# The first transform of a convolution's input taken from raw x with scaled matrices, and its neighbours moved

## The chip, the core and the metric

The kernel runs on one core of a Trainium2 chip. Five engines work side by side, each through its own list of instructions in order: TensorE (PE, with its weight loads shown as PEld), VectorE (DVE), ScalarE (ACT), GpSimd (POOL) and SyncE (SP), which here only starts transfers. The metric is the device time of one execution in microseconds (us).

## What is computed

A row of 640 channels and 2048 positions goes through a state-space convolution and a gated feed-forward part, each behind a layer norm whose scale and shift come from a conditioning vector:

```python
mod = (_silu(c) @ w_mod).reshape(c.shape[0], 6, 1, -1)      # sa, ca, ga, sb, cb, gb
h = _layernorm(x) * (1 + ca) + sa
x = x + ga * A(h)                        # A: y = causal convolution of h with K, plus h * D_skip
h = _layernorm(x) * (1 + cb) + sb
x = x + gb * B(h)                        # B: (silu(h w1) * (h w3)) w2, 1728 wide
# K[d, l] = 2 Re sum_n C[d, n] dt[d] exp(A[d, n] dt[d] l), n = 128
```

All arithmetic is in 32-bit floating point. The convolution is done by transforms of length 4096.

## The kernel before

The first part works on five blocks of 128 channels (b = 0 to 4). For each block:

- **The filter K** is generated in eight chunks of 16 channels (`gen_tasks`, `gen_chunk`). POOL adds integer phases (`ph`), three multiplications make magnitudes (tasks `z0` to `z2`, function `size`, on POOL), ACT takes sines (`tr`), DVE multiplies both (`xx`, `yy`), PE sums over n into the bank `kps`, four small matmuls add `D_skip` at one position (`kps<-dsk`), and ACT copies the bank to `ks`.
- **The input h** is made from x (`h_tasks`): four loads of raw x per block (`xq`), a normalisation by row (`hn<-xq`, on ACT or DVE), a multiplication by the gain row and an addition of the shift row on DVE (`hn<-hn,rw`, `hb<-hn,rw`), a store to the DRAM buffer `hs`, and a load back in another order (`xb<-hs`).
- **A first transform** of both (`first_tasks`): eight banks each of `ps<-wk,xb` for h and `ps<-wk,ks` for K, each bank copied by ACT or DVE into a spectrum `sp`.
- **A second transform** (`spectra_tasks`): `fh` for h, `fk` for K, eight banks each. ACT copies `fh` to `hz`, DVE multiplies the two spectra (`product`, `both`), PE goes back over frequencies (`fz`), and ACT or DVE copies that to `zt`, which is stored to the DRAM buffer `zd`.

The product has two forms, chosen by block in `FORM = "AABBB"`. In form A one DVE instruction of 1024 elements makes four partial products and PE adds them up with eight matmuls a bank pair; in form B two multiplications of 512, then a subtraction and an addition of 256 on DVE leave four matmuls.

After the last block comes a border. The last inverse transforms are read back from `zd` (`iz`, `izb`), summed with x by PE and DVE (`iy`, `iyb`), normalised and turned (`tp`), and the feed-forward part begins (`gu`, later `X`, `c`, `acc`), in two passes over 14 tiles of w1, w3 and w2.

The order of the first part and of the border is set by a table of numbers, `ORDER`: each number is a task and a mark behind it picks the second of two engines that may do it. Each engine executes its instructions in that order, and so does the queue of SP, through which nearly all transfers are started. The transfers of x for the second half of the rows (`x<-in_x` into `x2[2]` and `x2[3]`) and of two matrices `wd` are started at the head of `ffn`.

Of the kernel before, what the change touches and what calls it, by code (L numbers as in the profile page):

```python
# [18 lines left out]
P = 128  # L19
# [15 lines left out]
1 80 78 81 79 82 83 150' 2 4 19 42 20 41 14 21 15 84 22 43 23 44 16 85 151 24 17 25 26 45 46 18 28 59 47 30 27 29 48 96 33 36 49  # L35
34 5 111 35 32 61 31 37 40 50 51 38 39 3 152' 153 156 6 7 8 52 53 62 60 157 154 10 91 158 155 159 167 168 89 86 120 93 87 95 107
54 121 13 310 105 109 98 169 171 113 172 173 110 106 90 174 55 102 100 88 56 114 176 118 177 183 179 66 170 117 178 184 185 57 104
58 64 187 188 108 175 99 189 180 181 67 186 192 194 9 115 193 103 190 160 92 199 200 201 101 97 203 11 195 68 202 161 182 204 191
215 122 123 208 65 63 209 196 197 69 205 206 210 116 94 207 211 219 112 138 124 127 198 162 212 71 213 128 134 400' 119 163 125
# [3 lines left out]
267 338 334 259 339 315 265 266 405 260 268 77 335' 409 72 147 148 149 0 550 340 272 273 269 274 270 271 261 275 322 330 279 276  # L43
555 283 280 281 288 341' 551' 262 282 284 285 323 286 331 290 552 289 553 318 277 326 556 319 287 291 327' 417 421 418 422 278 320
321 423 292 557 426 545 316 293 137 410 75 74 546 424 419 558 420 427 317' 428 547 548 328 413' 414 324 429 425 294 329 430 433
437 325 346 342 344 554 559 436 434 442 435 431 347 438 444 343 345' 443 348 350 365 352 439 549 440 441 432 445 449 450 451 452
# [4 lines left out]
505 496 517 1054 394 583' 510 570 518 515 654 652 529 516 530 531 574 810 373 809 1055 571 533 511 584 524 523 1056 522 572 575  # L51
519 811' 812 813 1058 1057 384 532 656' 539 585 512 520 534 573 535 538 525 540 576 395 1059 577 521 396 1060 588 1061 398' 566
1063 814 589' 536 537 567 526 1064' 1065 1066 568 580 569' 527 578 908 909 581 579 528 657 655 658 659 660 667 683 668 684 661 685
669 541 592 593' 542 1311 594 671 1068 1069' 676 1070 595 672 543 590 544 670 678 677 596 673 674 591 662 663 686 664 910 665 1071
815 597 586 820 675 679 587' 680 1062 1067 1072 687 821' 692 1312 1313 1314 699 824 598 681 818 600 1316 1315 825 688 693 819' 694
# [3 lines left out]
730 752 753 608 399 630 826 744 745 618 757 756 827 754 631 755 619 641 759 750 763 764 758 620' 760 766 765 767 768 746 769 770  # L59
# [13 lines left out]
1221 1127 907 1222 1122 1124 1125 1340 1341 1214 1223 1116 1228 1227 1128 1141 1229 1234 1232 1179' 1233 1177 1117 1129 1130 1119  # L73
# [132 lines left out]
class K:  # L206
# [1139 lines left out]
    def ffn(self):  # L1346

        W, X, v, w2 = self.first
        for b in (2, 3):
            self.load_x2(b)  # L1350
# [766 lines left out]
```

## Time and profile before

| | |
|---|---|
| time, median of 3 runs | 954.85 us (951.83 to 956.61) |
| span of the profiled execution | 950.6 us; the page gives no other time for it |
| busy: PE, DVE, ACT, POOL | 868.3, 684.2, 549.9, 342.1 us |
| instructions: PE, DVE, ACT, POOL | 8369, 1294, 1035, 371 |
| first `fh` of block 0 | 111.8 us |
| first matmul of the feed-forward part (`gu`) | 380.5 us |

How to read it: the first 380 us are the convolution, in which all four engines have work, and the remaining 570 us are the feed-forward part. A 32-bit matmul of the program stands as two records in the profile. A duration is from start to end of one instruction, and neighbours on an engine overlap a little, so a sum of durations is somewhat longer than the busy time.

### The profile page before, as it was taken

How to read it: one execution, taken by the hardware profiler on the slowest of the kernel's cores; microseconds unless marked ns; L12 is line 12 of the kernel's file. 1: busy time of each engine (PE TensorE's matmuls, PEld its weight loads, DVE VectorE, ACT ScalarE, POOL GpSimd, SP SyncE). 2: the span in 40 equal slices, each digit the busy share in tenths (PEclk: the TensorE clock that was granted, in tenths of full speed). 3: DMA queues.
4: the chain of work that ended last, by engine and by line, in shares of the span. 5: the costliest groups of instructions: out<-in, count | busy, mean ns of one | idle time of the engine just before them, and what ended most of it. 6: DMA issues, size and time to landing. Idle time of an engine off the chain costs nothing.

```text
span 950.6 us, 21218 instructions
## 1 busy us (share of the span) xinstructions
PE 868.3 (91%) x8369; PEld 686.4 (72%) x8369; DVE 684.2 (72%) x1294; ACT 549.9 (58%) x1035; POOL 342.1 (36%) x371
## 2 busy tenths in 40 slices
PE   1267999999999986999999999999999999999997
PEld 0035858777888863787777778888788888888775
DVE  7997999999989878896776775657556555555422
ACT  6688999989797732754444444544444444443412
POOL 0899989998998500011111211000121212120000
PEclk9997999999999997999999999999999999999999
DMA  9976553524143598654533422375432222221374
GB/s 201 266 225 171 158 150 107 138 80 127 47 119 84 143 241 209 170 175 149 154 113 121 139 67 87 94 238 171 126 92 83 83 84 83 84 84 31 111 230 127
DMA packets 110508, 127.42 MB, mean 134 GB/s; under 512 B 10568, under 2 KB 90696, under 8 KB 109128
## 3 DMA queue, kind: packets, MB, share of 16 engines
q1 hardware_dynamic: 109032, 125.27, 46.7%
q8 instruction: 66, 1.08, 0.5%
q10 hardware_dynamic: 1376, 0.79, 0.3%
q14 instruction: 34, 0.28, 0.1%
HBM read 95.89 MB, written 30.15 MB: 133 GB/s over the span
## 4 chain that ended last, share of the span: by engine, by line
PE 73%; DVE 9%; ACT 8%; DMA 5%; issue 2%; POOL 1%; SPq 1%; ACTq 0%; DVEq 0%; POOLq 0%
PE c L151 19%; PE acc L151 18%; PE X L151 12%; PE ps L151 5%; PE kps L151 4%; PE fz L151 4%; PE fk L151 3%; PE fh L151 3%; PE gu L151 2%; ACT tr L151 1%; DVE xb L151 1%; PE iy L151 1%; DMA sp<-zd 1%; DMA zd<-zt 1%; DVE yy L151 1%
## 5 line engine op out<-in xcount | busy, mean ns | idle before, releaser
L151 PE MATMUL acc<-ah,w 128*128 128x512 f32 x560 | 173.4, 395 | 1.9 <-DMA w<-w2d 1.2
L151 PEld LDWEIGHTS acc<-ah,w 128*128 128x128 f32 x560 | 103.8, 188 | 25.3 <-ACT ah L598 1.8
L151 PE MATMUL acc<-al,w 128*128 128x512 f32 x260 | 102.3, 393 | 0.0
L599 DVE TENSOR_TENSOR wl<-s,wh 128x256 fp32r<-128x256 f32 x92 | 39.0, 424 | 67.0 <-ACT wh L598 66.5
L775 POOL TENSOR_TENSOR s<-wr 128x256 f32<-128x256 f32 x22 | 16.4, 743 | 184.8 <-DMA wr<-in_w 104.7
L598 ACT ACTIVATE wh<-s 128x256 fp32r<-128x256 f32 x92 | 37.6, 409 | 78.0 <-PE X L151 58.1
L151 POOL TENSOR_TENSOR ph<-p,p 128x1024 int32<-128x1024 int32 x40 | 78.8, 1970 | 6.2 <-ACT tr L151 5.6
L598 ACT ACTIVATE wh<-wr 128x256 fp32r<-128x256 f32 x92 | 38.4, 418 | 56.1 <-PE X L151 42.4
L776 POOL TENSOR_TENSOR s<-s,wr 128x256 f32<-128x256 f32 x22 | 17.1, 776 | 131.5 <-issue 128.0
L151 DVE TENSOR_TENSOR yy<-yy,tr 128x512 f32<-128x512 f32 (+1 forms) x60 | 56.5, 944 | 2.9 <-ACT tr L151 2.1
L836 ACT ACTIVATE t<-g 128x512 f32<-128x512 f32 x44 | 27.8, 632 | 52.9 <-DVE g L800 52.9
L151 PEld LDWEIGHTS acc<-al,w 128*128 128x128 f32 x260 | 48.9, 188 | 11.3 <-DVE al L599 0.4
L151 ACT ACTIVATE tr<-ph,hpi 128x512 f32<-128x512 f32 x80 | 54.5, 688 | 3.3 <-DVE yy L151 1.3
L151 DVE TENSOR_TENSOR xx<-tr,xx 128x512 f32<-128x512 f32 x80 | 54.2, 681 | 2.9 <-ACT tr L151 2.5
L805 DVE SCALAR_TENSOR_TENSOR g<-t,g 128x512 f32<-128x512 f32 x48 | 33.7, 701 | 31.3 <-ACT t L836 29.3
L151 PE MATMUL kps<-yy,xx 128*32 128x64 f32 x1920 | 37.8, 231 | 18.3 <-DVE xx L151 14.2
L151 PE MATMUL fz<-fp,wz 64*128 64x512 f32 x224 | 54.0, 608 | 0.3 <-DVE fp L151 0.3
L151 PEld LDWEIGHTS kps<-yy,xx 128*32 128x32 f32 x1920 | 32.8, 114 | 27.1 <-issue 11.1
L599 DVE TENSOR_TENSOR wl<-wr,wh 128x256 fp32r<-128x256 f32 x92 | 40.2, 438 | 15.1 <-ACT wh L598 15.0
L151 PE MATMUL ps<-wk,xb 128*64 128x128 f32 x640 | 47.2, 294 | 2.8 <-DVE hb L151 1.1
L151 ACT ACTIVATE tr<-ph 128x512 f32<-128x512 int32 x80 | 47.2, 599 | 2.3 <-DVE yy L151 1.8
L598 ACT ACTIVATE ah<-h 128x512 fp32r<-128x512 f32 x26 | 16.4, 632 | 53.1 <-PE acc L151 53.1
(454 smaller groups left out, 2442.3 us busy)
## 6 DMA issues: line engine op xcount, KB each, us to landing
w<-w2d SPq DMA_DIRECT2D x42, 640.0 KB, 3.9
wr<-in_w SPq DMA_DIRECT2D x50, 320.0 KB, 3.9
zd<-zt SPq DMA_DIRECT2D x40, 256.0 KB, 3.2
w2d<-w SPq DMA_DIRECT2D x14, 640.0 KB, 3.5
xs<-in_x SPq DMA_DIRECT2D x16, 320.0 KB, 11.9
hs<-hb SPq DMA_DIRECT2D x20, 256.0 KB, 3.2
xb<-hs SPq DMA_DIRECT2D x20, 256.0 KB, 4.8
iz<-zd SPq DMA_DIRECT2D x32, 160.0 KB, 4.2
```

The source lines that it names most:

```text
L151: self.prev = self.k.order(f(*a, **kw), self.prev)
L598: self.nc.scalar.activation(H, v, AF.Copy)
L599: eng.tensor_tensor(Lo, v, H.bitcast(F32), op=ALU.subtract)
L775: eng.tensor_tensor(s[0], u[:, 0:2], u[:, 2:4], op=ALU.add)
L776: eng.tensor_tensor(s[1], s[0], g[:, 0:2], op=ALU.subtract)
L805: V.scalar_tensor_tensor(g, th, 1.0, g, op0=ALU.add, op1=ALU.mult)
L836: tanh = lambda o, i: A.activation(o, i, AF.Tanh, scale=0.5)
```

## The change

- **h from raw x.** `h_norm`, `h_mul` and `h_add` are gone. Raw x is the moving operand of PE, 32 positions at a time, and the transform matrix is multiplied by the rows' 1/std (`hw`, `hl`; tasks `hw0`, `hw1`, `hl0`, `hl1`, once for all blocks). A second, accumulating matmul adds the mean and the shift. Each of the 20 tasks `h{b}.{i}.m` issues 32 matmuls (`hp`), on four groups of 32 rows of the array, into two banks. ACT or DVE copies each bank to `hb`, two transfers store it to `hs`, and four loads per block bring the result straight to the place of the spectrum. There are no banks `ps<-wk,xb` and no copies of them.
- **The gain** of block 0 is multiplied to x on DVE (four instructions). For the other blocks it goes into K's parameters and into `D_skip` (tasks `mv`, `gain`, `pr`, `rw` instead of the rows and `fold`).
- **The skip per half block.** Ten small additions on POOL or DVE (`g{b}.d0`, `g{b}.d1`) replace the matmuls `kps<-dsk`. The first transform of K waits for them, so for four chunks at a time.
- **Form B for all blocks.** `FORM` is `"BBBBB"`.
- **Two engines to choose from** for `z0` to `z2` (14 of 120 are on DVE now) and for the head of a table.
- **The border.** The loads `izb` are all started by SP (half of them were by ACT). `x2[2]` and `wd[2]` are loaded as tasks of the border, `x2[3]` and `wd[3]` within the first pass.
- **A new `ORDER`** for all of it.

```diff
@@ -32,67 +32,66 @@
 ORDER = """
-1 80 78 81 79 82 83 150' 2 4 19 42 20 41 14 21 15 84 22 43 23 44 16 85 151 24 17 25 26 45 46 18 28 59 47 30 27 29 48 96 33 36 49
...
+1 2 6 79 81 3 82 20 15 5 83 85 84 21 16 43 154' 42 80 22 155 23 24 17 25 18 19 115 44 29 7 31 62 45 30 32 60 26 9 40 157 27 46 158 8
...
-FORM = "AABBB"
+FORM = "BBBBB"
...
-    def h_make(self, pc, b):
+    def h_first(self, pc, b, bank):
...
         for j in range(4):
+            for n in range(2):
+                for g in range(4):
+                    p, q = slice(32 * g, 32 * g + 32), 64 * (g % 2)
+                    self.nc.tensor.matmul(bank[g // 2][q:q + 64, j * P:j * P + P], (self.hl if n else self.hw)[p, 4 * b + j, :],
+                                          self.hr[p, pc * P:pc * P + P] if n else x[p, j, :], start=(n == 0), stop=(n == 1),
+                                          skip_group_check=True, tile_position=(32 * g, q))
+    def h_store(self, pc, b, c):
+        hb = self.hb.pop((pc, b, c))
+        to = self.hs[pc].rearrange("f (g s) d -> g f s d", g=4)
+        for q in range(2):
+            self.nc.sync.dma_start(to[2 * c + q, :, 4 * b:4 * b + 4], hb[64 * q:64 * q + 64].rearrange("p (s d) -> p s d", s=4))
...
-            for q in range(4):
-                g = slice(32 * q, 32 * q + 32)
-                nc.tensor.matmul(kps.rearrange("p (e b) -> p e b", b=64)[g, :, 63], self.ident[g, g], self.dsk[g, d0 // P, d0 % P // 4:d0 % P // 4 + 4],
-                                 start=False, stop=True, skip_group_check=True, tile_position=(32 * q, 32 * q))
...
+        def skip(e, h):
+            k = self.ks[b][:, 16 * h:16 * h + 16, 63]
+            self.eng(e).tensor_tensor(k, k, self.dsk[:, b, 16 * h:16 * h + 16], op=ALU.add)
...
-                add(n + f"z{i}", "POOL", 1.03, lambda c=c, i=i: ch[c][1](i), [n + "ph", f"exp{b}"] + ([f"mag{b}"] if i == 2 else [n + "z0"] if i else []),
+                add(n + f"z{i}", ("POOL", "DVE"), (1.03, .6), lambda e, c=c, i=i: ch[c][1](e, i), [n + "ph", f"exp{b}"] + ([f"mag{b}"] if i == 2 else [n + "z0"] if i else []),
...
-            add(n + "n", ("ACT", "DVE"), (1.89, 1.66), lambda e, i=i, place=place: self.h_norm(b, i, place(), e), [n + "l", "hscale"], t, take=[(bank, 1)],
-            add(n + "x", "DVE", .61, lambda i=i: self.h_mul(b, i), [n + "n", "fold"], t + .1)
-            add(n + "a", "DVE", .61, lambda i=i: self.h_add(b, i), [n + "x"], t + .2, take=[("hz", 1)], give=[(bank, n + "n")])
+            add(n + "m", "PE", 1.95, lambda i=i: mm(i), [n + "l", "rw0", "rw1", "hw0", "hx0", "hx1"] + ([n + "x"] if b == 0 else []), t + .2,
+            for c in range(2):
+                add(n + f"e{c}", ("ACT", "DVE"), (.48, .61), lambda e, i=i, c=c: self.h_out(b, i, c, pk[i][c], e), [n + "m"], t + .2, take=[("hz", 1)],
...
+            add(f"h{b}.f{k}", "SP", 0, lambda k=k: self.h_fetch(b, k), [f"h{b}.{i}.o{c}" for i in range(4) for c in range(2)] + old, W["h"](b, 4), dma=[524288])
...
-                    (self.nc.scalar if h else self.nc.sync).dma_start(z["b", b][h * 64:h * 64 + 64, pr], zv[:, t0:t0 + 4, cut:])
+                    self.nc.sync.dma_start(z["b", b][h * 64:h * 64 + 64, pr], zv[:, t0:t0 + 4, cut:])
```

Three places of the order carry the prediction. **The first** is PE at the first `fh` of block 0. Before, it stands behind the ninth chunk of K (`kps`) in the program's order:

```order
L151 MATMUL ps_1227<-wk,ks_133 64x4x16x2 x8
L151 MATMUL ps_1236<-wk,ks_133 64x4x16x2 x8
L151 MATMUL ps_1245<-wk,ks_133 64x4x16x2 x8
L151 MATMUL kps_1260<-x_94,xx_1098 32x64 x32
L151 MATMUL kps_1260<-dsk,ident 32x4 x4
L151 MATMUL fh_1304<-sp,wb 64x128 x8
L151 MATMUL fk_1313<-sp,wb 64x128 x8
```

In the change it stands behind the eleventh chunk, between two tasks that already transform h of block 1 (`hp`, weights from `xb`, moving operand `xq` or the row `rw`):

```order
L154 MATMUL hp<-xq_1353,xb 64x128 x4
L154 MATMUL hp<-rw,xb 64x128 x4
L154 MATMUL kps_1492<-yy_1136,xx_1135 32x64 x32
L154 MATMUL fh_1534<-sp,wb 64x128 x8
L154 MATMUL fk_1548<-sp,wb 64x128 x8
L154 MATMUL hp<-xq_1399,xb 64x128 x4
L154 MATMUL hp<-rw,xb 64x128 x4
```

So the second transform of block 0 has moved two chunks later, and work of block 1 ahead of it. **The second** place is DVE among the products of block 0. Before, form A's product of 1024 elements stands beside the arithmetic of h (`hn`, `hb`) and the sines' products (`yy`, `xx`):

```order
L151 TENSOR_TENSOR fp_1588<-fk_1517,hz_1577 128x4x256
L151 SCALAR_TENSOR_TENSOR yy_1529<-yy_1529,tr_192_1579 128x16x32
L151 TENSOR_TENSOR yy_1529<-yy_1529,tr_192_1579 128x16x32
L151 TENSOR_TENSOR hn<-hn,rw 128x512
L151 TENSOR_TENSOR xx_1528<-tr_192_1599,xx_1528 128x512
L151 TENSOR_TENSOR hb_1626<-hn,rw 128x512
```

In the change a product of block 0 is two multiplications and two sums, and a magnitude (`xx<-late`) that POOL made before stands among them:

```order
L154 TENSOR_TENSOR fp_1607<-fk_1548,hz_1557 128x2x2x128
L154 TENSOR_TENSOR fk_1548<-fk_1548,hz_1557 128x2x2x128
L154 TENSOR_TENSOR fp_1607<-fp_1607,fk_1548 128x256 x2
L154 SCALAR_TENSOR_TENSOR yy_1487<-yy_1487,tr_192_1600 128x16x32
L154 TENSOR_TENSOR yy_1487<-yy_1487,tr_192_1600 128x16x32
L154 TENSOR_TENSOR xx_1612<-late 128x512
```

The arithmetic of h has left DVE here, and more of the products' work has come to it. **The third** is the queue of SP at the border. Before, behind the last store of `zd`, it starts two of the four loads of each `izb` (ACT starts the others), a weight tile and then x:

```order
L151 DMA izb_5365<-zd 64x4x128 x2
L151 DMA izb_5395<-zd 64x4x128 x2
L151 DMA wr_1_5400<-in_w 128x5x128 x2
L594 DMA x_5384<-in_x 32x2560 x4
L594 DMA x_5385<-in_x 32x2560 x4
```

In the change it starts all eight, with a weight row between the two groups:

```order
L154 DMA izb_5546<-zd 64x4x128 x4
L154 DMA w2r_5587<-in_w 128x640
L154 DMA izb_5600<-zd 64x4x128 x4
L154 DMA x_5584<-in_x 32x2560
L154 DMA wr_1_5613<-in_w 128x5x128
```

The loads of x are spread out behind it, and four starts of `izb` have moved from ACT to SP.

More of the change, by code (lines that the diff above doesn't have):

```diff
@@ L1300, in tail_tasks @@
         load_down(2)
+        add("lwd2", "SP", 0, lambda: self.nc.sync.dma_start(self.wd[2], self.t_wd[:, 8:12]), ["change"], -20, dma=[262144])
+        for q in range(4):
+            s = slice(q * 32, q * 32 + 32)
+            add(f"lx2.{q}", "SP", 0, lambda q=q, s=s: self.nc.sync.dma_start(self.x2[2][s], self.xv[q, :, 8:12, :]), ["border"], -20, dma=[327680])
         down_split(2, 60)
@@ L1359, in groups @@
             more = m < 12
+            if p == 0 and m == 4:
+                self.load_x2(3)
             if more:
@@ L1548, in border @@
             self.x2 += [self.fp.tile([P, 4, D], F32, name=f"x2{i}") for i in (2, 3)]
-        plan.add("change", None, 0, change, [f"g{b}.7.p", f"g{b}.7.r"] + [f"h{b}.{i}.x" for i in range(4)], 0, own=True)
+        plan.add("change", None, 0, change, [f"g{b}.7.p", f"g{b}.7.r"], 0, own=True)
         self.tail_tasks(border, cut)
@@ L1920, in param_tasks @@
             if k:
-                c = chain(f"pc{k}.", end, n, {0: [b]}, prio + .3 + k * later)
+                c = chain(f"pc{k}.", end, n, {0: [b], len(end) - 1: ["gain"]}, prio + .3 + k * later)
             else:
@@ new lines, in early_tasks, with spread @@
+        add("mv", "PE", .4, columns, ["m"], 21, take=[("f2", 1)], give=[("hz", "m")])
+        add("gain", "DVE", 1.6, gain, ["mv", "dt", "hc"], 21, give=[("f2", "mv")], port=True)
+        def spread(i):
+            o = pr["r", i] = ps.tile([P, 512], F32, name=f"prow{i}", tag="f", bufs=3)
+            for k in range(4) if i == 0 else (4,):
+                for g in range(4):
+                    nc.tensor.matmul(o[32 * g:32 * g + 32, k % 4 * P:k % 4 * P + P], gc[:, k], self.ident, start=True, stop=True, tile_position=(0, 32 * g))
+            if i:
+                nc.tensor.matmul(o[:, P:2 * P], bc(gc[:, 0, 0], 1, P), self.ident, start=True, stop=True)
+                for q in range(4):
+                    g = slice(32 * q, 32 * q + 32)
+                    nc.tensor.matmul(o[g, 2 * P:3 * P], hc[g, 65:97], de[g].rearrange("p b e -> p (b e)"), start=True, stop=True, tile_position=(32 * q, 32 * q))
@@ new lines, in keep @@
+        def keep(i):
+            if i == 0:
+                return A.activation(rwf[:, :512], pr["r", 0], AF.Copy)
+            A.activation(rwf[:, 512:768], pr["r", 1][:, :256], AF.Copy)
+            A.activation(self.dsk[:, 1:].rearrange("p b e -> p (b e)"), pr["r", 1][:, 256:384], AF.Copy)
+        for i in range(2):
+            add(f"pr{i}", "PE", .9, lambda i=i: spread(i), ["gain"], 21, take=[("f2", 1)])
+            add(f"rw{i}", "ACT", .55, lambda i=i: keep(i), [f"pr{i}"], 21, give=[("f2", f"pr{i}")])
@@ new lines, in rows_of, with ends @@
+        def rows_of(i):
+            V.tensor_tensor((self.hw, self.hl)[i], bc(self.h_rs[i], 2, 64), bc(hc[:, :64], 1, NJ), op=ALU.mult)
+        for i in range(2):
+            add(f"hw{i}", "DVE", 1.13, lambda i=i: rows_of(i), ["hscale", "hc", "pc0", "pc1.8"], 21)
+        pl = {}
+        def ends(i):
+            pl[i] = ps.tile([P, 512], F32, name=f"hl{i}", tag="f", bufs=3)
+            for g in range(4):
+                p = slice(32 * g, 32 * g + 32)
+                for n, (o, r) in enumerate(((65, self.hl[p, 8 * i:8 * i + 8]), (64, bc(hc[p, :64], 1, 8)))):
+                    nc.tensor.matmul(pl[i][p], hc[p, o:o + 32], r, start=(n == 0), stop=(n == 1), skip_group_check=True, tile_position=(32 * g, 32 * g))
@@ L2062, in early_tasks, with lower @@
+        def lower(i):
+            A.activation(self.hl[:, 8 * i:8 * i + 8], pl[i].rearrange("p (j c) -> p j c", j=8), AF.Copy)
+        for i in range(2):
+            add(f"hl{i}", "PE", 1.0, lambda i=i: ends(i), ["hw1"], 21, take=[("f2", 1)])
+            add(f"hx{i}", "ACT", .48, lambda i=i: lower(i), [f"hl{i}"], 21, give=[("f2", f"hl{i}")])
+        add("wb", "SP", 0, lambda: nc.sync.dma_start(self.wb, self.t_wb), ["mr4", "lat1", "turn0", "turn1"], 60, dma=[2097152])
         w = {}
```

252 lines of the change are left out of this document (125 added, 127 removed), and 66 rows, old and new, of the table ORDER.

## The prediction

> **What bounds the kernel now.** I read the span first, then the busy time by stage, cut where PE starts a chunk of K: the ninth, the 25th and the last of the forty.
>
> ```profile
> span 950.6 us, 21218 instructions
> 110.54 1.17 PE L151 MATMUL kps<-x,xx 128*32 128x64 f32 x64
> 235.03 1.17 PE L151 MATMUL kps<-yy,xx 128*32 128x64 f32 x64
> 327.69 1.17 PE L151 MATMUL kps<-yy,xx 128*32 128x64 f32 x64
> ```
>
> The columns of the next rows are the stretch, its length, the busy time of PE, its weight loads, DVE, ACT and POOL, the granted clock, and the DMA share.
>
> ```profile
> 0.00:83.90 83.90, 31.27 (x465) 17.02 (x465) 73.69 (x151) 64.64 (x127) 55.80 (x71) 0.94 0.83 225
> 83.90:110.54 26.64, 24.21 (x497) 21.50 (x489) 23.61 (x40) 24.34 (x45) 25.50 (x27) 0.94 0.63 169
> 110.54:235.03 124.49, 118.74 (x2371) 94.09 (x2369) 117.84 (x171) 116.74 (x199) 113.36 (x111) 1.00 0.45 119
> 235.03:327.69 92.66, 92.09 (x2074) 77.45 (x2073) 86.15 (x144) 76.59 (x133) 80.40 (x76) 1.00 0.35 94
> 327.69:354.20 26.51, 24.02 (x384) 19.39 (x385) 18.27 (x37) 9.87 (x20) 0.00 (x0) 1.00 0.98 232
> 354.20:380.50 26.30, 17.85 (x94) 10.07 (x93) 21.09 (x73) 5.93 (x10) 0.63 (x1) 0.74 0.89 211
> ```
>
> From 110 to 235 us PE is busy 95%, DVE 95%, ACT 94% and POOL 91%: nothing is slack, and an engine that gets faster alone gains little. From 235 to 328 us PE is full (99%) with DVE at 93% behind it. Before 84 us PE is mostly idle and DVE leads (88%). Behind 380.5 us comes the feed-forward part, 570 us that the change does not touch but for transfers started elsewhere. So the gain, if there is one, is made between 84 and 328 us, and it needs less work on PE and on DVE at once. What DVE waited for from 100 to 330 us was small:
>
> ```profile
> DVE fp L151 <- PE fk L151: 4.3, 8, 1.3
> DVE yy L151 <- ACT tr L151: 2.6, 7, 0.8
> DVE xx L151 <- ACT tr L151: 1.9, 4, 1.4
> ```
>
> **What the change does to PE.** These rows show the matmuls that go, and what stands next, so that start to start gives the cost on PE.
>
> ```profile
> 129.43 3.70 PE L151 MATMUL fz<-fp,wz 64*128 64x512 f32 x16
> 133.06 1.13 PE L151 MATMUL fh<-sp,wb 128*64 128x128 f32 x16
> ...
> 198.19 1.17 PE L151 MATMUL kps<-yy,xx 128*32 128x64 f32 x64
> 199.29 0.24 PE L151 MATMUL kps<-dsk,ident 32*32 32x4 f32 x8
> 199.46 1.15 PE L151 MATMUL fk<-sp,wb 128*64 128x128 f32 x16
> 200.43 1.18 PE L151 MATMUL ps<-wk,xb 128*64 128x128 f32 x16
> 201.55 1.17 PE L151 MATMUL kps<-x,xx 128*32 128x64 f32 x64
> ...
> 238.89 1.99 PE L151 MATMUL fz<-fp,wz 64*128 64x512 f32 x8
> 240.81 2.06 PE L151 MATMUL fh<-sp,wb 128*64 128x128 f32 x32
> ```
>
> - Form B in blocks 0 and 1: an inverse transform takes 133.06 - 129.43 = 3.63 us in form A and 240.81 - 238.89 = 1.92 us in form B. Eight of them change: 8 x 1.71 = **-13.7 us**.
> - The skip: 199.46 - 199.29 = 0.17 us per chunk, 40 chunks: **-6.8 us**.
> - h's first transform: forty banks at 201.55 - 200.43 = 1.12 us go, 45 us, and twenty tasks `hp` of 32 matmuls, 64 records, come. No row shows four groups of 32 rows with long moving operands. Two rows bound it, and two show how much runs side by side:
>
> ```profile
> L151 PE MATMUL fz<-fp,wz 64*128 64x512 f32 x224 | 54.0, 608 | 0.3 <-DVE fp L151 0.3
> L151 PE MATMUL ps<-wk,xb 128*64 128x128 f32 x640 | 47.2, 294 | 2.8 <-DVE hb L151 1.1 <-DVE fp L151 0.6 <-DVE sp L151 0.6
> L151 PE MATMUL kps<-dsk,ident 32*32 32x4 f32 x320 | 9.7, 180 | 0.0
> ```
>
>   `ps` works on two halves of the array's columns: 16 records in 1.12 us are 8 steps of 0.14 us. `fz` works on two halves of its rows, in different banks; 224 records of 608 ns in 54.0 us, so neighbours overlap. With four row groups at once a task `hp` is 16 steps, 16 x 0.14 = 2.2 us. It can't be less than 1.1 us, in which the 64 records of a `kps` are issued, and with only two groups at once it is 32 x 0.14 = 4.5 us. I take 2.2 us, as the two row groups of `fz` are nearest: 20 x 2.2 = 44 us for 45, **-1 us** (ends -23 and +45).
>
> The gain's small matmuls replace four of the same kind where PE is idle: 0. Sum for PE: **-21 us**.
>
> The Trainium skill bears on `hp` in TensorE: Matmul & The Clock Gate, section Why this matters for your kernels: four tiles of 32 rows ran concurrently and gained 3.07 times, not four. By that a task would be an estimated 2.2 x 4 / 3.07 = 2.9 us and PE's sum -8 us. No run here shows it yet.
>
> **What it does to DVE, ACT and POOL.** Counts are those of the two programs, durations are the rows' means.
>
> ```profile
> L151 DVE TENSOR_TENSOR fp<-fk,hz 128x1024 f32<-128x1024 f32 x16 | 19.5, 1218 | 1.4 <-PE fk L151 1.1 <-ACT hz L151 0.3
> L151 DVE COPY sp<-ps 128x512 f32<-128x512 f32 x28 | 18.9, 681 | 2.9 <-PE ps L151 2.7
> L151 DVE TENSOR_TENSOR fp<-fp,fk 128x256 f32<-128x256 f32 x48 | 17.9, 415 | 0.5
> L151 DVE TENSOR_TENSOR fp<-fk,hz 128x512 f32<-128x512 f32 x24 | 16.5, 688 | 9.4 <-PE fk L151 8.0 <-ACT zt L151 0.9 <-ACT wh_u L151 0.3
> L151 DVE TENSOR_TENSOR hn<-hn,rw 128x512 f32<-128x512 f32 x20 | 13.9, 693 | 0.4
> L151 DVE TENSOR_TENSOR hb<-hn,rw 128x512 f32<-128x512 f32 x20 | 13.7, 686 | 0.5
> L151 DVE TENSOR_SCALAR hn<-xq,rs_y_h,rs_n_h 128x128 f32<-128x128 f32 x28 | 11.5, 412 | 0.9
> L151 DVE TENSOR_SCALAR step<-pS 128x128 int32<-128x128 int32 x3 | 0.7, 270 | 0.0
> ```
>
> DVE loses 32 normalisations (the 28 shown and four like them, 13.2 us), the multiplications and additions of h (27.6), sixteen products of form A (19.5), eleven of 28 copies to `sp` (7.5) and some 5 us of smaller work: 73 us. It gets sixteen pairs of form B's multiplications (32 x 0.69 = 22.0) and 32 sums (32 x 0.415 = 13.3), 14 magnitudes from POOL (9.6), seven copies of `hp` (4.8), 25 shifts of tables less four (some 5), four multiplications of x (2.8), two of the transform matrix (2.4), and some 18 tiny instructions of `gain`, between 0 and 0.4 us each, at the shifts' 0.27 us 5 us. Sum 65 us: **-8 us** (ends -13 and -6).
>
> ```profile
> L151 ACT ACTIVATE sp<-ps 128x512 f32<-128x512 f32 x52 | 30.0, 590 | 9.8 <-PE ps L151 9.7
> L151 ACT ACTIVATE hn<-xq,rs_n_h,rs_y_h 128x128 f32<-128x128 f32 x36 | 16.6, 461 | 1.0
> L151 POOL TENSOR_TENSOR yy<-late 128x512 f32<-128x512 f32 x22 | 23.2, 1074 | 0.0
> ```
>
> ACT loses 48 normalisations at 0.461 us (22) and 29 copies to `sp` at 0.59 (17) and gets 33 of `hp` (19.5): about **-19 us**. POOL loses 14 magnitudes at 1.074 us and heads of tables: **-15 us** or more. Its ten skip additions of 16 elements are bounded by zero and the head's magnitude, 1 us each; I take 0.3 us.
>
> **How it adds up.** DVE has the smallest saving among four engines that are all nearly full. If DVE stays as busy as it was, the stretch is 8 us shorter; if PE could stay as busy as it was, 21 us. DVE is the nearer row, and its waits for PE's `fk` (4.3 us) and half of those for sines (2.2) should go with PE's and ACT's relief: 8 + 6.5 = **14.5 us** earlier at the last chunk.
>
> Given back: the last block's K waits for the skip behind its eighth copy, about 0.5 us with nothing behind it on POOL by then; three more banks of K's transform stand behind the last chunk, with two fewer of `fh`, about 1 us. At the border the chain runs from the last store through `izb` to `iyb`:
>
> ```profile
> 350.89 7.92 SPq L151 DMA_DIRECT2D zd<-zt  x5
> 362.92 2.56 SPq L151 DMA_DIRECT2D izb<-zd  x4
> 366.36 0.40 PE L151 MATMUL iyb<-izb,late 128*64 128x128 f32 x2 [2.82 <-DMA izb<-zd]
> ```
>
> Four starts take SP 2.56 us, 0.64 each. The first `izb` had two from SP and two from ACT, and now has four from SP: +1.3 us on that chain. The second comes 3.2 us later, which the first one's normalisation covers. The loads of x leave the busy stretch behind `izb`, but PE's one wait for transfers there is for `izb`, started ahead of them: 0, between -2.8 us (that wait) and nothing. More transfers for h (100 instead of 40 by count) meet a DMA share of 0.35 to 0.45 and an SP that mostly waits for others: 0; if SP fell behind, each would cost its 0.64 us.
>
> Total -14.5 + 0.5 + 1 + 1.3 = -11.7 us. Made on the profiled execution: 950.6 - 11.7 = 938.9 us of span. The three timed runs have a median of 954.85 us, 4.2 us over that span; I count this as what lies around it. **Forecast 943 us.**
>
> **The rivals.**
>
> - *The row groups do not run four at a time* (slower). Groups 0 and 1 of `hp` write the same bank, groups 2 and 3 the other. If two groups on one bank take turns, a task is 4.5 us and PE's sum is -21 + 45 = +24 us; block 0's four tasks lie where PE still has gaps, so 36 of the 45 count: about +15 us, **970 us**. It decides from about 3.3 us a task on, where PE's saving is used up. For it: `fz`, the only long row-split matmul, uses a bank for each half. Against it: `kps<-dsk` put four row groups into one bank, 320 records of 180 ns in 9.7 us, so several at once, though with four columns only. Chance 0.13.
> - The Trainium skill has this as a rule in TensorEngine Tiling (Array Packing), section Restrictions and Gotchas: different row tiles can't access the same PSUM bank at the same time. By that rule the 970 us would be the time; the `dsk` row speaks against it, weakly.
> - *Hidden* (no change). The first `fh` moves from the ninth to the eleventh chunk, and between the last `hp` of block 0 and it lie a store and a fetch through DRAM. The statistics of the rows end later in DVE's order too. If PE stood idle there for some 12 us, all would be used up: **954 us**. Against it: `hp` of block 1 and banks of K stand there to be done. Chance 0.14.
> - *PE alone decides* (more gain). If DVE's instructions fit into PE's schedule, the stretch shrinks by PE's 21 us: 950.6 - 21 + 2.8 = 932.4 of span, **936 us**. Against it: DVE at 95% with only 8 us less. Chance 0.13.
>
> **How the numbers follow.** The forecast has 0.60, with 937 to 949 us of its own, from the ends of DVE's sum and of its waits. The range holds it, the larger gain and the hidden case: 931 to 957 us, leaving out the slower rival. A measurement of this kernel tells about 0.5% from no change, so faster is below 950.1 us and slower above 959.6: faster 0.60 + 0.13 = 0.73; same 0.14; slower 0.13.
>
> **What would show it.** Right: a task `hp` advances PE by about 2.2 us; the last chunk of K starts near 313 us instead of 327.7; DVE is busier than PE from 110 us on; `gu` starts near 369 us. Wrong: `hp` above 3.3 us a task; PE idle for over 5 us ahead of the first `fh`; an `iyb` wait longer than the 2.8 us before.

## The result: the main stretch shrank, the start grew by more

The changed kernel takes 969.66 us (median of 4 runs, 966.33 to 972.49) where the kernel before took 953.34 beside it: a ratio of 1.0154, 95% interval 1.0122 to 1.0185. By that ratio it is slower by about 15 us, where 12 us of gain were forecast. Its profiled execution has a span of 964.5 us.

The cut that explains it has four stages: the start, divided at 84 us, up to the first `fh` (the first matmul on the spectrum of h); from there to the first `gu` (the convolution's main stretch and the border); and the feed-forward part. First the busy time by stage of the kernel before; the columns are those of the prediction's table.

```profile
0.00:84.00 84.00, 31.37 (x467) 17.10 (x469) 73.79 (x151) 64.64 (x127) 55.90 (x71) 0.94 0.83 225
84.00:111.81 27.81, 25.38 (x560) 22.58 (x561) 24.78 (x42) 25.58 (x47) 26.67 (x28) 0.95 0.65 177
111.81:380.50 268.69, 251.44 (x4852) 199.84 (x4845) 242.07 (x419) 207.90 (x360) 193.12 (x186) 0.97 0.51 130
380.50:950.60 570.10, 560.14 (x2502) 446.87 (x2500) 343.57 (x685) 251.81 (x502) 66.38 (x88) 1.00 0.40 121
```

The same four stages of the changed kernel:

```profile
0.00:84.00 84.00, 31.74 (x535) 21.66 (x539) 74.22 (x148) 57.00 (x112) 52.05 (x62) 0.90 0.74 200
84.00:136.63 52.63, 35.96 (x826) 25.95 (x818) 42.17 (x80) 41.10 (x64) 40.62 (x37) 0.84 0.43 125
136.63:391.18 254.55, 231.11 (x4856) 184.03 (x4853) 220.50 (x406) 183.69 (x318) 168.43 (x162) 0.96 0.71 177
391.18:964.50 573.32, 560.30 (x2502) 446.85 (x2500) 343.21 (x686) 251.74 (x502) 65.56 (x88) 1.00 0.41 122
```

The second column is the length. The main stretch went from 268.69 to 254.55 us, **14.1 us shorter**. The first `fh` starts at 136.63 instead of 111.81, **24.8 us later**. The feed-forward part went from 570.10 to 573.32, **3.2 us longer**. Together +13.9, the difference of the two spans. Up to 84 us PE was busy as long in both; from 84 us to the first `fh` it was busy 25.38 of 27.81 us before and 35.96 of 52.63 now. Nearly all of the 14.1 us lies ahead of the last chunk of K: from the first `fh` to it there are 215.9 us before and 201.9 now.

The granted clock in these rows differs too: 0.95 before and 0.84 now between 84 us and the first `fh`.

The lines of the changed kernel that answer to those of the prediction's steps, from the timeline of PE: the last chunk of K, and a task `hp` of block 1 from its first record to what follows it.

```profile
138.57 0.45 PE L154 MATMUL hp<-xq,xb 32*64 32x128 f32 x8
...
140.47 0.77 PE L154 MATMUL fh<-sp,wb 128*64 128x128 f32 x10
...
338.52 1.16 PE L154 MATMUL kps<-yy,xx 128*32 128x64 f32 x64 [1.17 <-DVE xx L154]
```

A task `hp` takes 140.47 - 138.57 = 1.9 us, against 2.2 in the forecast; thirteen of the twenty tasks take 1.90 to 1.97. The task right ahead of the first `fh` takes 4.07 us (131.46 to 135.53), and there the granted clock is 0.58, where it is 1.00 at 138.57. So some 2 us of the later start are a lower clock at this one task. The last chunk starts at 338.5, not 313. The groups of PE:

```profile
L154 PE MATMUL fz<-fp,wz 64*128 64x512 f32 x160 | 41.0, 614 | 2.5 <-DVE fp L154 2.5
L154 PE MATMUL hp<-rw,xb 32*64 32x128 f32 x640 | 36.9, 283 | 0.0
L154 PE MATMUL hp<-xq,xb 32*64 32x128 f32 x512 | 31.1, 290 | 2.2 <-ACT hb L154 1.4 <-issue 0.3 <-ACT hz L154 0.2
```

`fz` fell from 54.0 to 41.0 us (13.7 were forecast). The groups of `hp` run side by side, so their sums overlap.

**What is late at the start.** From the timelines, the row scale's end on DVE (`rs_n_h`) and the fetch of block 0's spectrum on SP, before:

```profile
64.99 0.17 DVE L151 SCALAR_TENSOR_TENSOR rs_n_h<-h_nm,rs_y_h 128x16 f32<-128x16 f32 x1
...
84.35 2.23 SPq L151 DMA_DIRECT2D xb<-hs  x4
```

And in the changed kernel, with the first multiplication of the scaled matrix, the sixteen stores of block 0 and the fetch:

```profile
96.28 1.55 DVE L154 SCALAR_TENSOR_TENSOR rs_n_h<-h_nm,rs_y_h 128x16 f32<-128x16 f32 x1
99.55 1.21 DVE L154 TENSOR_TENSOR xb<-rs_n_h,hc 128x1024 f32<-128x1024 f32 x1
...
112.41 0.45 PE L154 MATMUL hp<-sp,xb 32*64 32x128 f32 x8
...
115.14 13.05 SPq L154 DMA_DIRECT2D hs<-hb  x16
...
130.50 0.39 SPq L154 DMA_DIRECT2D sp<-hs  x1
```

Before, the fetch left SP at 84, some 27 us ahead of the first `fh`, so h was early and the chunks of K ended the start. Now the fetch leaves only at 130.5. Yet the first `fh` does not wait for it. PE's rows show what it waited for:

```profile
100.91 1.95 PE L154 MATMUL hl<-xb,hc 32*32 32x512 f32 x8 [8.49 <-DVE xb L154]
...
130.37 1.16 PE L154 MATMUL kps<-yy,xx 128*32 128x64 f32 x64 [3.00 <-POOL x L154]
131.46 0.48 PE L154 MATMUL hp<-xq,xb 32*64 32x128 f32 x6
...
135.53 1.17 PE L154 MATMUL kps<-yy,xx 128*32 128x64 f32 x64
136.63 1.09 PE L154 MATMUL fh<-sp,wb 128*64 128x128 f32 x16
```

The longest wait, 8.5 us, belongs to h: `hl` makes part of the scaled matrix. Two others, 3.0 and 2.1 us, are chunks of K that wait for POOL. From 130.37 on PE waits for hardly anything, and `fh` stands behind the eleventh chunk. So h and the chunks of K end the start together.

### The profile page after: what moved, and what is told of

Same layout as the page of the kernel before. It is cut to its first block, busy times and chain, and to the rows that moved or that the text cites. A ratio compares the mean times of both kernels' runs of the same rounds, so it can differ in the third digit from the quotient of the medians.

```text
span 964.5 us, 21975 instructions
## 1 busy us (share of the span) xinstructions
PE 859.1 (89%) x8707; PEld 678.5 (70%) x8707; DVE 680.1 (71%) x1317; ACT 533.5 (55%) x994; POOL 326.7 (34%) x348
## 4 chain that ended last, share of the span: by engine, by line
PE 63%; DVE 12%; ACT 8%; DMA 7%; POOL 4%; issue 3%; SPq 2%; DVEq 0%; ACTq 0%; POOLq 0%
PE c L154 19%; PE acc L154 17%; PE X L154 12%; PE hp L154 3%; DVE yy L154 2%; ACT tr L154 2%; DVE fp L154 2%; PE kps L154 2%; PE gu L154 2%; SPq L154 2%; PE fh L154 2%; DMA x<-in_x 2%; POOL ph L154 1%; PE fz L154 1%; DVE xx L154 1%
## 5 line engine op out<-in xcount | busy, mean ns | idle before, releaser
L154 PE MATMUL ps<-wk,ks 128*64 128x128 f32 x640 | 43.3, 294 | 8.5 <-POOL ks L154 3.3
L154 PEld LDWEIGHTS ps<-wk,ks 128*64 128x64 f32 x640 | 38.6, 148 | 14.6 <-POOL ks L154 3.5
```

The source lines that it names most:

```text
L154: self.prev = self.k.order(f(*a, **kw), self.prev)
```

## The experiments

One table first. For each kernel: its median, the ratio to the kernel before measured beside it with its 95% interval, and, from its one profiled execution, the start of the first `fh`, the time from there to the first `gu`, and from there to the end. Profiled starts of kernels that are alike up to there differ by some 4 us.

| kernel | us | ratio | first `fh` | `fh` to `gu` | `gu` to end |
|---|---|---|---|---|---|
| before | 953.3 | 1 | 111.8 | 268.7 | 570.1 |
| changed | 969.7 | 1.0154 (1.0122-1.0185) | 136.6 | 254.6 | 573.3 |
| e_ring | 962.6 | 1.0092 (1.0061-1.0124) | 141.1 | 248.2 | 573.5 |
| e_hst | 969.9 | 1.0171 (1.0125-1.0217) | 135.6 | 257.4 | 573.3 |
| e_ring_hst | 961.9 | 1.0085 (1.0055-1.0116) | 133.9 | 249.9 | 573.4 |
| e_zpool | 967.0 | 1.0126 (1.0089-1.0162) | 135.2 | 257.9 | 573.6 |
| e_all | 961.4 | 1.0076 (1.0051-1.0101) | 136.6 | 249.5 | 573.4 |
| e_noscale | 967.8 | 1.0148 (1.0103-1.0193) | 137.5 | 254.3 | 573.7 |
| e_banks | 969.2 | 1.0160 (1.0134-1.0187) | 137.7 | 253.2 | 574.2 |
| e_border | 969.5 | 1.0167 (1.0140-1.0195) | 138.2 | 257.0 | 572.8 |
| e_izb | 971.5 | 1.0185 (1.0162-1.0208) | 140.3 | 256.2 | 573.8 |
| e_forma | 976.8 | 1.0241 (1.0205-1.0277) | 136.9 | 264.9 | 573.7 |
| e_dsk | 977.4 | 1.0245 (1.0193-1.0296) | 143.6 | 255.2 | 573.1 |
| e_stats2 | 979.8 | 1.0278 (1.0254-1.0302) | 149.8 | 256.1 | 573.3 |
| e_stats | 984.6 | 1.0318 (1.0290-1.0346) | 152.2 | 259.0 | 573.1 |
| e_old | 1068.1 | 1.1201 (1.1182-1.1221) | 153.4 | 338.7 | 574.4 |
| e_old_ring | 1070.8 | 1.1230 (1.1197-1.1263) | 152.6 | 343.1 | 575.7 |
| b_formb | 961.6 | 1.0086 (1.0058-1.0114) | 113.6 | 277.9 | 571.0 |
| b_skip | 978.0 | 1.0265 (1.0226-1.0304) | 119.6 | 286.4 | 570.2 |
| b_formb_skip | 985.5 | 1.0333 (1.0299-1.0366) | 119.0 | 295.5 | 570.3 |

**Two groups of rows in one bank (e_banks).** The slow rival's time, 970 us, came out; this run tests its mechanism.

```diff
-                    p, q = slice(32 * g, 32 * g + 32), 64 * (g % 2)
-                    self.nc.tensor.matmul(bank[g // 2][q:q + 64, j * P:j * P + P], ...
+                    p, q = slice(32 * g, 32 * g + 32), 64 * (g // 2)
+                    self.nc.tensor.matmul(bank[g % 2][q:q + 64, j * P:j * P + P], ...
```

> The changed kernel with the two banks of hp dealt out otherwise: row groups 0 and 2 write one bank, 1 and 3 the other, so that neighbours in the stream never write the same bank; the stores follow. If groups that share a bank take turns, a task hp gets shorter than the 1.9 us it advances PE now, towards 1.1 us, and the time falls by up to 20 x 0.8 = 16 us less what waits elsewhere. If they don't, it stays at 1.9 us and the time within 1 us, ratio 1.015.

969.2 against 969.7: nothing. Two groups still share each bank here, so this says only that the pairing does not matter. The 1.9 us of a task decide: the slow rival needed more than 3.3. It is out, and that its 970 us was hit is chance.

**The staging buffers (e_ring).** What ACT and others waited for between 84 and 330 us in the changed kernel (total, times, longest):

```profile
POOL ph L154 <- ACT tr L154: 14.9, 9, 3.0
ACT hb L154 <- DMA hs<-hb: 11.1, 9, 3.8
DVE yy L154 <- ACT tr L154: 9.1, 5, 3.0
POOL ks L154 <- ACT ks L154: 7.5, 3, 4.6
ACT hz L154 <- DMA hs<-hb: 5.1, 5, 1.8
```

The ring `hz` has three buffers, and each of the forty banks of h now holds one until its two stores have landed. ACT stands 16.2 us for that, with the sines (`tr`) queued behind it, for which DVE and POOL wait. The edit gives block 0 four buffers, the other blocks three of their own, and pays with half a product tile that form B doesn't use.

```diff
-        return self.core.tile([P, 512], F32, name=name, tag="hz", bufs=3)
+        return self.core.tile([P, 512], F32, name=name, tag="hz", bufs=4)
...
-        hb = self.hb[pc, b, c] = self.ring(f"hb{pc}{b}{c}")
+        hb = self.hb[pc, b, c] = self.fpool.tile([P, 512], F32, ..., tag="hb", bufs=3) if pc else self.ring(f"hb{pc}{b}{c}")
```

> The changed kernel with more staging buffers: the tile of a product is halved (form B uses only its first half), the ring hz has 4 buffers instead of 3, and hb of blocks 1 to 4 gets a ring of its own of 3. No instruction and no order differs. Theory R (a bank of hb holds a buffer of hz until its store has landed, so ACT stands still and the sines come late): ACT's waits for hs<-hb, 16.2 us in 84 to 330 us, fall below 3 us, DVE's waits for tr there from 17.5 to about 8 us, the last chunk of K comes 5 to 9 us earlier than 338.5 us, ratio to before 1.005 to 1.010 instead of 1.0154. Theory S (the late row statistics cause it): ACT's waits go too, but the last chunk moves by under 2 us and the ratio stays at 1.013 or more.

962.6. The same waits in it:

```profile
POOL ph L154 <- ACT tr L154: 10.4, 8, 5.0
...
ACT hb L154 <- DMA hs<-hb: 1.3, 2, 0.8
...
DVE yy L154 <- ACT tr L154: 0.7, 2, 0.5
```

ACT's waits for the stores are gone, as expected. Not all waits fell with them: those of DVE for sines, over all its tiles, went from 17.5 to 12.2 us, not to 8, and ACT's wait of `hb` for `hp` rose from 5.0 to 13.4. The last chunk of K starts at 336.67, 1.9 us earlier and not 5 to 9, since this profiled start is 4.5 us later; counted from the first `fh` it comes 6.3 us earlier.

The gain repeats in another pair of kernels that differ by the rings alone, 969.9 (e_hst) to 961.9 (e_ring_hst), near the 962 to 963 expected if both edits relieve the same buffers (959.5 if not). From 967.0 (e_zpool) to 961.4 (e_all) the split stores come in as well. So some 7 us of the loss are the staging buffers, and they are gained in the main stretch, which is 248 to 250 us long in these kernels. In the order of e_old the rings gain nothing (e_old_ring, below).

**Parts taken back: the border (e_border, e_izb).** e_border starts the loads of x and `wd` at the head of the feed-forward part again; e_izb lets ACT start half of `izb` again.

```diff
-                    self.nc.sync.dma_start(z["b", b][h * 64:h * 64 + 64, pr], zv[:, t0:t0 + 4, cut:])
+                    (self.nc.scalar if h else self.nc.sync).dma_start(z["b", b][h * 64:h * 64 + 64, pr], zv[:, t0:t0 + 4, cut:])
```

> The changed kernel with x2[2], x2[3] and wd[2], wd[3] loaded again at the head of the feed-forward part as before the change. Theory B (the moved loads cost the 2.5 us that lie between gu and the first acc): gu to the first acc falls from 27.1 to about 24.6 us, ratio 1.0125 to 1.013. Rival: the 2.5 us come from izb and the transposes ahead of them and not from x; then 27 us and 1.015 stay.

> The changed kernel with half of the izb loads started by ACT again, as before the change. Theory Q (SP starts eight loads in a row, and the second half of the rows comes too late for x4h and x5h): gu to the first acc falls from 27.1 to 24.6 us, and gu comes 1.3 us earlier; ratio 0.2 to 0.4% lower than 1.0154. Rival: the second half waits for DVE's statistics; both stay within 0.5 us.

969.5 and 971.5: neither gains anything. The 3.2 us of the feed-forward part remain in both. Every kernel with the new tasks has about as much (572.8 to 575.7), every one built on the kernel before is at 570.2 to 571.0.

**The statistics earlier (e_stats, e_stats2).** Only the order differs; e_stats also moves the sums of squares and the loads for the gain.

```diff
 place in the order, e_stats2
-mean3 289  hscale 296  hw1 312  hl0 315  h0.3.m 339  h0.f0 409
+mean3 263  hscale 264  hw1 267  hl0 277  h0.3.m 319  h0.f0 390
```

> The changed kernel with another ORDER: the sums of squares on ACT, the row scale (hscale), hw, hl and the four tasks of block 0's first transform stand earlier, the table of exponentials of block 2 later; nothing else. Theory S (block 0's h is late because the statistics stand late in the order of DVE and ACT, and PE has too little to do meanwhile): the last sum of squares ends near 65 us instead of 83.3, hw starts before 88 us instead of 99.6, PE's wait of 8.5 us at hl is gone, the last chunk of K comes 6 to 12 us earlier than 338.5, ratio 1.002 to 1.009. Theory R (the staging ring): the last chunk moves by under 3 us, ratio 1.012 or more.

> The changed kernel with only the row scale (mean3, hscale, hw) moved ahead on DVE to where its last input is ready, hl, hx and block 0's hp with it, and the exponentials of block 2 behind them on ACT; all sums of squares and loads stay. Theory S: hp of block 0 starts 6 to 10 us earlier than 112.4 us, the last chunk of K 3 to 8 us earlier than 338.5, ratio 1.007 to 1.012. Rival: DVE's other work (the sixth and seventh chunk) only takes the place of the row scale, hp starts earlier and fh does not; ratio 1.013 to 1.018.

Both miss: 984.6 and 979.8. The rows of e_stats, from the timelines of DVE, PE and SP:

```profile
68.99 0.50 DVE L154 SCALAR_TENSOR_TENSOR rs_n_h<-h_nm,rs_y_h 128x16 f32<-128x16 f32 x1
...
96.58 0.43 PE L154 MATMUL hp<-sp,xb 32*64 32x128 f32 x4 [0.16 <-ACT xb L154]
...
125.78 1.87 PE L154 MATMUL pv<-ident,mc 128*128 128x4 f32 x8 [6.68 <-ACT mc L154]
...
126.54 1.01 SPq L154 DMA_DIRECT2D sp<-hs  x2
...
145.32 1.96 PE L154 MATMUL kps<-yy,xx 128*32 128x64 f32 x64 [7.52 <-ACT ks L154]
...
152.17 1.09 PE L154 MATMUL fh<-sp,wb 128*64 128x128 f32 x16
```

The row scale ends 27 us earlier and `hp` starts 16 us earlier, and yet `fh` is 15 us later. The fetch of h leaves SP at 126.5, some 26 us ahead of `fh`: h is early here, and the chunks of K, which stand ahead of `fh` in PE's order, end the start. PE's long waits there are for ACT: 6.7 us at `pv` and 7.5 at a chunk, whose bank waits for a copy (`ks`).

**h's chain shortened (e_hst, e_noscale) and DVE relieved (e_zpool).** e_hst starts every second store of block 0 on ACT. e_noscale leaves out the three Newton steps of the row scale. e_zpool gives five magnitudes (`g0.3.z0`, `g0.6.z2`, `g1.1.z0`, `g1.2.z2`, `g1.3.z1`) from DVE to POOL; their marks in `ORDER` go.

```diff
-            self.nc.sync.dma_start(to[2 * c + q, ...
+            (self.nc.scalar if pc == 0 and q else self.nc.sync).dma_start(to[2 * c + q, ...
...
-        for i in range(3):
+        if work:
+            nc.vector.tensor_copy(y, w)
+        for i in range(0 if work else 3):
...
 ORDER
-443' 271' 461' 476' 220'
+443 271 461 476 220
```

> Block 0's sixteen stores of h (13.05 us on SP, two starts per bank) are started half by SP and half by ACT; no order and no arithmetic differ. Theory 1 (the end is set by the chain from the row scale over hl, hp and the stores to the first fh): the sixteen stores span 9 to 10 us, the first fh starts about 3 us earlier than 136.63, gu too, about 966.5 us (ratio to the changed kernel 0.997). Theory 2 (a bank's two stores hold its staging buffer, and ACT stands behind it): ACT's waits for hs<-hb at 116 to 126 us (2.6 us) go, same sign, 2 to 3 us. Rival (a start costs ACT as much as SP, 0.6 us each, and ACT is the late engine there): ACT loses 5 us and the ninth and tenth chunk come later, 970 to 975 us.

> The row scale of h leaves out its three Newton steps on DVE (12 instructions at 93.7 to 96.2 us, about 2.4 us; one copy comes instead) and uses the first estimate of one over the standard deviation; nothing else differs. Theory 1 (the chain from the row scale to the first fh sets the end): fh and gu 2 to 2.4 us earlier, 967 us or a little more below. Theory 3 (DVE's whole work before the first fh sets it, not this chain): the same 2.4 us, but chunk 8's product (112.81) comes earlier by as much too. Rival (another chain sets it: loads, the modulation's columns): nothing, 969.7.

> In the changed kernel five of the magnitudes (the first multiplication of a table pair, yy or xx from e, between 54 and 131 us) go from DVE back to POOL, at the same places of the order; they take DVE 6.4 us now (2.52 of it at 54.14). Nothing else differs. If DVE's own work ahead of the first fh delays it (116 us busy of 136.6 in the changed kernel against 98.6 of 111.8 before): fh 3 to 6 us earlier, 964 to 967. If POOL is as late there and has no gap where they fall: slower, 972 to 980. If neither: 969.7.

e_hst gives nothing (969.9), e_noscale 1.9 us and e_zpool 2.7, each within what its interval leaves. No single piece of the start that was tried holds the 25 us, as is to be expected where h and the chunks of K end it together.

**One part alone, in either order (e_forma, e_dsk, b_formb, b_skip, b_formb_skip).** e_forma and e_dsk take form B and the skip out of the changed kernel; the three others put them into the kernel before, each new instruction right behind what it needs.

```diff
-FORM = "BBBBB"
+FORM = "AABBB"
...
+            for q in range(4):
+                g = slice(32 * q, 32 * q + 32)
+                nc.tensor.matmul(kps.rearrange("p (e b) -> p e b", b=64)[g, :, 63], self.ident[g, g], ...
...
-                add(f"{g}.d{c // 4}", ("DVE", "POOL"), (.1, .12), lambda e, h=c // 4: skip(e, h), ...
```

> The changed kernel with form A back in blocks 0 and 1 (the sixteen sums on DVE go, PE does four steps of an inverse for two); everything else in its place. If PE sets the stretch from 140 to 235 us: up to 13.7 us slower, 975 to 983. If DVE does: up to 16 us faster, 954 to 965. If waits for sines and staging set it, both stay hidden: 968 to 971.

> The skip goes back into PE: four matmuls per chunk (kps<-dsk), and the ten additions on POOL with their waits go; the rest of the changed kernel's order stays. If the prediction's term holds (40 x 0.17 us of PE saved): PE's busy time to gu grows by 6 to 7 us and, since PE is full from 200 us on, the time grows by 4 to 7 us, 974 to 977. If the additions cost more than they save (POOL waits 7.5 us for ACT ks ahead of them, with the next chunks' tables queued behind): 960 to 967. If both are hidden: 969.7.

> One part alone: the kernel before with form B in blocks 0 and 1 too, each sum put right behind its multiplications on DVE; everything else in its place. PE loses 8 x 1.71 = 13.7 us, DVE gains 22.0 + 13.3 - 19.5 = 16 us net. Theory PE (the prediction's terms for PE can be cashed in one by one): faster, to 940 to 948 us. Theory DVE (from 110 to 235 us DVE is as late as PE, 95 % busy): up to 16 us slower, 955 to 970 us, and the sign of the term is wrong by itself.

> One part alone: the kernel before with the skip added per half block by POOL (ten additions behind the fourth and eighth copy of a block), the four small matmuls per chunk gone; the transforms of K of a half wait for it. If the term holds: PE loses 6.8 us, 946 to 949 us. If the wait on POOL or DVE's fullness eats it: 953.

> Both parts in the kernel before: PE loses 20.5 us, DVE gains 16. If PE's terms add: 933 to 942. If DVE is as late: about what form B alone gives, less at most 6.8. Against the changed kernel (969.7) the remainder is what h's new transform and the new order cost.

Form B costs 8 us in the kernel before (961.6) and saves 7 in the changed one (976.8 without it). Its main stretch in the kernel before, and then the changed kernel's with form A:

```profile
113.64:391.49 277.85, 244.32 (x4789) 199.09 (x4781) 253.41 (x467) 207.93 (x360) 192.98 (x186) 0.96 0.49 124
```

```profile
136.87:401.73 264.86, 241.23 (x4920) 186.17 (x4917) 209.75 (x358) 184.86 (x318) 168.32 (x162) 0.97 0.67 170
```

In b_formb PE works 7.1 us less (251.44 to 244.32) and DVE 11.3 more (242.07 to 253.41), and the stretch grows by 9.2: it follows DVE. In e_forma DVE works 10.8 us less (220.50 to 209.75) and PE 10.1 more (231.11 to 241.23), and the stretch grows by 10.3: it follows PE. This fits a stretch that was bound by DVE before and is bound by PE now, where form B is worth about what the prediction gave it. It is not fully shown: each order was made for its own form, and no order was made for the exchanged one.

The skip is not as clear. Taken back, it costs 7.7 us, near the 6.8 of the forecast, but in the profile 7.0 of it lie ahead of the first `fh` and 0.6 in the main stretch, where the matmuls saved were expected to count. In the kernel before the same part costs 25 us, placed right behind the fourth and the eighth copy: there POOL waits 20.2 us in all for ACT's copies (`ks`) between 84 and 330 us, with its next work queued behind. Both parts together (b_formb_skip) cost 32 us, more than either theory allowed. What the skip is worth depends on where POOL gets to it.

**All tasks in the old order (e_old).** The changed kernel's tasks stand in the order of the kernel before, as far as they have the same names.

```diff
 place in the order
-hscale 296  hw1 312  h0.3.m 339  h0.f0 409  g0.4.p 229  g0.7.p 336
+hscale 175  hw1 216  h0.3.m 225  h0.f0 301  g0.4.p 264  g0.7.p 358
```

> The changed kernel's tasks in the order of the kernel before: tasks that both have stand in the old sequence and on the old engines (all magnitudes on POOL), the new ones where their predecessors stood (hp at the normalisation, its copies at the multiplication and the addition, hw and hl at the old fold). Theory O (the edits are worth what their instructions say and the new ORDER loses it): first fh before 118 us, the last chunk of K before 330 us, time at or below before, ratio 0.985 to 1.003. Rival W (the work itself is what costs: two stores and two copies for one, a longer chain to h): fh later than 125 us and the ratio stays at 1.01 or more, in whatever order.

1068.1 us: `fh` at 153.4 and a ratio far above 1.01, as rival W expected. Larger rings don't help it (e_old_ring, 1070.8, where 4 to 7 us less were expected if the stores cost as much in any order). The new order recovers some 98 us of what the new tasks cost in an order not made for them.

**What was gained back together (e_all).** Rings, split stores and magnitudes:

> The larger staging rings, the split starts of block 0's stores and the five magnitudes on POOL together. If the magnitudes give what they promise, on top of 962: 956 to 959, still no less than the kernel before (953). If POOL is as late: 965 to 972.

961.4 us, 1.0076 (1.0051 to 1.0101): no more than the rings alone. No kernel here beats the one before.

```profile
136.58:386.13 249.55, 227.75 (x4857) 180.03 (x4853) 223.30 (x408) 184.24 (x319) 170.04 (x164) 0.97 0.71 182
```

Its main stretch is 249.55 us, 19.1 less than before, more than used up by the first `fh` at 136.6, 24.8 us later, and the 3.3 us at the end.

## Why the prediction failed, step by step

- **The step that failed** is in "How it adds up": "If DVE stays as busy as it was, the stretch is 8 us shorter", carried over to the last chunk as "14.5 us earlier". The sum was made over the whole convolution, as if the stretch began at the same time. Counted from the first `fh`, the last chunk did come 14.0 us earlier, but the stretch began 24.8 us later, so the chunk came 10.8 us later. And that 14.0 is so near to 14.5 is luck. In this stretch DVE's work fell by 22.6 us (202.71 to 180.07) and not by 8. Its waits for `fk` fell from 4.3 to 1.1 us, much as forecast, but its waits for sines, which were to fall by 2.2, rose from 4.5 to 14.0.
- **DVE's term.** Eight microseconds less was forecast; the stages above give 73.79 + 24.78 + 242.07 = 340.6 before and 74.22 + 42.17 + 220.50 = 336.9 now, 3.7 less. The mis-sized row is that of the fourteen magnitudes from POOL: 9.6 us were forecast, their groups sum to 16.0 (five `yy<-e,e` and `xx<-e,e` take 8.6 of it, beside POOL's work). More than the size, the split was missed: 21.6 us less behind the first `fh` and 17.8 more ahead of it. Two more chunks stand there now (five multiplications each, some 3.9 us by their rows); the rest, some 10 us, is what the gain, the scaled matrices, the multiplications of x and nine of the magnitudes (12.3 us) add, less the normalisation and arithmetic of h that stood there (12.8 us). Removed work lay late (the normalisations of all blocks), added work early (once for all blocks).
- **The rival named "Hidden"** came nearest: it had PE idle ahead of the first `fh`, by some 12 us, and named the row statistics that end later in DVE's order. The idle time of PE there grew by 13.9 us (111.81 - 56.75 = 55.06 before, 136.63 - 67.70 = 68.93 now). What it lacked are some 11 us more in which PE is busy ahead of the first `fh`, partly at a lower clock. Its store and fetch are not what PE waits for; behind the last `hp` of block 0, `hp` of block 1 and banks of K do stand there to be done. The reason against it failed further ahead: PE waits 8.5 us at `hl` for the scaled matrix, with chunks of K queued behind it. PE idle for over 5 us there was a sign of being wrong that the prediction had named.
- **"More transfers for h ... 0"** was wrong by some 7 us. SP kept up; but the price was put on SP's starts, and it lies in the three staging buffers that the transfers hold.
- **`hp`** was right in kind and cheaper than taken, where the clock is full: 1.9 us a task for 2.2. **The slow rival** is refuted by this. The Trainium skill's rule in TensorEngine Tiling (Array Packing), Restrictions and Gotchas, that different row tiles can't access one PSUM bank at the same time, does not show here: groups 0 and 1 share a bank on different halves of its partitions, and a task still takes 1.9 us. No run gives each group a bank of its own. Nor does the estimate of 2.9 us show, worked out from the Trainium skill's TensorE: Matmul & The Clock Gate, Why this matters for your kernels; the row says 1.9.
- **Form B**, -13.7 us: `fz` fell by 13.0, and e_forma puts its worth at 10.3 us of the stretch. Right, probably because DVE was relieved at the same time; the prediction's plain sum of PE's terms would have credited it in the kernel before too, where it costs 8 us.
- **The skip**, -6.8: e_dsk agrees in size (7.7), not in place.
- **"PE alone decides"** (21 us) was the better forecast for the stretch alone: with larger rings it is 18.8 to 20.5 us shorter. Its whole time missed the start like the forecast.
- **At the border** the loads cost nothing, as forecast, and all of `izb` on SP nothing that shows (1.3 forecast). Between the first `gu` and the end 3.2 us came that no step had. In the trace DVE reaches the second half's statistics later there, here before and then now, with what PE waits for:

```profile
384.21 0.73 DVE L151 BATCH_NORM_AGGREGATE mv<-st 128x2 f32<-128x30 f32 x4
```

```profile
396.80 0.72 DVE L154 BATCH_NORM_AGGREGATE mv<-st 128x2 f32<-128x30 f32 x4
...
405.59 0.51 PE L154 MATMUL gu<-x4h,wh_u 128*128 128x512 f32 x1 [1.47 <-ACT x4h L154]
406.78 0.50 PE L154 MATMUL gu<-x4l,wh_u 128*128 128x512 f32 x1 [0.69 <-DVE x4l L154]
```

  384.21 is 3.7 us behind the first `gu`, 396.80 is 5.6, and the first `acc` comes 27.1 us behind `gu` instead of 24.6. In e_old, where DVE has the old order, `acc` comes after 25.2, but 3.6 us are lost further on. So the order of DVE is a likely cause, read from the traces, and not a settled one.

What stays open: how much of the 24.8 us is work that any order must do ahead of the first `fh`, how much is this order, and how much is the lower clock, of which only the 2 us at one `hp` are read off. Moving h's work ahead by hand made it worse, and shortening single pieces gave 0 to 3 us. No other order was searched for.

## What to carry to other kernels

Make the sum stage by stage, with the start as a stage of its own: work that is removed from every block and work that is added once, ahead of the first, do not cancel, even where the totals do. A saving on one engine has a price only beside the engine that sets the stretch; the same edit cost 8 us in one kernel and saved 7 in the other. Where an engine's result now leaves through a transfer, count how long each staging buffer is held, and who is queued behind the engine that waits for one.

## What the runs showed of the hardware

The four row groups of `hp`, two to a bank, issue 64 records in 1.9 us, though a single record takes 0.28. The same task took 4.07 us where the granted clock was 0.58.

DVE's time for one and the same instruction can depend on POOL. `rs_n_h`, 128x16, took 0.17 us at 64.99 in the kernel before and 1.55 us at 96.28 in the changed one. POOL's timeline of the changed kernel there:

```profile
95.85 1.95 POOL L154 TENSOR_TENSOR e<-al,j 128x1024 f32<-128x1024 f32 x1
```

It ends at 97.80, and DVE's instruction at 97.83. A magnitude on DVE behaves alike, 0.68 us at one place and 2.52 at another:

```profile
43.66 0.68 DVE L154 TENSOR_TENSOR yy<-e,e 128x512 f32<-128x512 f32 x1
...
54.14 2.52 DVE L154 TENSOR_TENSOR yy<-e,e 128x512 f32<-128x512 f32 x1
```

In both cases POOL worked beside it. At 43.67 it was POOL's `xx<-e,e` that took 1.58 us instead of 1.06. At 54.16 POOL's `ph` took 1.95 us, to 56.11, and DVE's multiplication ended 0.55 us behind it, at 56.66. These places agree with the Trainium skill, SBUF — State Buffer (section SBUF: two separate sides), which calls the port pair that the two engines share an exclusive lock held for a whole instruction. Not every small instruction is held up: beside the same `e<-al,j`, two steps of the row scale on 128x16 elements took 0.18 and 0.17 us, at 95.85 and 96.07, and `rs_n_h` at 64.99 in the kernel before began beside a `ph` of POOL (63.17 to 65.12). What decides between the two is not shown here.
